# Loading the K cache in runs of 32 KB per partition instead of 16 KB, in a decode kernel that streams its KV cache

## The chip, the cores and the metric

The kernel runs on one core of one Trainium2 chip. The metric is device time in microseconds (us), the median of several executions. Most executions of one kernel agree within 0.3%. Each run is compared with the kernel before as measured beside it, on the same chip.

Engine names: PE is the matrix engine (PEld its weight loads), DVE, ACT and POOL the other compute engines, SP the engine whose queue issues nearly all loads. A core has 16 DMA engines; "DMA" in a profile means these together. L417 is line 417 of the kernel file.

## The reference

One decode step of a transformer block: adaLN modulation, attention of one query row over a cache of 65,536 positions (32 query heads, 4 KV heads, head size 128), output projection, and a GEGLU FFN. Cut to what matters here:

```python
q = (h @ wq)                                  # 1 x 4096: 32 heads of 128
scores = einsum('bhqd,bhkd->bhqk', q, k) * 128 ** -0.5
p = softmax(scores)
o = einsum('bhqk,bhkd->bhqd', p, v)           # k, v: [1, 4, 65536, 128] bf16, each shared by 8 query heads
```

K and V are 67 MB each, the weights another 51 MB. Every byte is read once, so the kernel is a stream of loads with arithmetic beside it. Softmax doesn't care in which order positions are visited, as long as K and V are visited alike.

## The kernel before

Partition p of the SBUF holds 512 consecutive positions of a KV head. The attention has 32 steps. Each takes 64 positions of every partition, which is a run of 64 x 128 x 2 bytes = 16 KB per partition, 2 MB per load. There are ten SBUF buffers of that size ("slots"): K uses 0 to 3, V uses 4 to 7; slots 8 and 9 serve weights only.

```python
SLOT = 8192          # bf16 elements of a partition: 16 KB
NSLOT = 10
SITES = 4            # K buffers, and V buffers
CH = 64              # positions of a partition in a step
...
    for i in range(NC + 2):                                  # NC = 32 steps
        if i < NC:
            j_k[i] = plan_load(kv_src(kh, i), kv_view, i % SITES, kfill[i % SITES])
        if i >= 2:
            j = i - 2
            j_v[j] = plan_load(kv_src(vh, j), kv_view, SITES + j % SITES, vfill[j % SITES])
```

Loads are issued in this planned order and never overtake each other. A load is issued when the work that last used its buffer has ended:

```python
def issue_ready():
    while issued[0] < len(loads):
        j = loads[issued[0]]
        if j.prev is not None:
            if j.prev.freed is None:
                return
            SP.wait(j.prev.freed)
        sp.dma_start(j.view, j.src).then_inc(j.tok[0], 16)
        issued[0] += 1
```

A step i on PE transposes the K of step i (`T`, 4 groups of 16), multiplies the K of step i-1 with the query (`QK`), and multiplies the probabilities of step i-2 with their V (`PV`):

```python
def T(b):
    ...
    if b == 0:
        pwait(kfill[s], i, it)               # this step's K has landed
    ...                                      # 16 transposes into kt_ps (L417)
    if b == NB - 1:
        release(j_k[i], pt[("T", i, b)])     # K buffer free after the last transpose

def PV(q):
    j = i - 2
    ...
    if q == 0:
        pwait(vfill[s], j, it)               # V of step i-2 has landed
    ...                                      # 16 products into b7 (L481)
    if q == NB - 1:
        release(j_v[j], pt[("PV", j)])       # V buffer free

T(0); QK(0); T(1); QK(1); PV(0); T(2); QK(2); QK(3)      # one step (written on
PV(1); T(3); PV(2); MT(); PV(3); MB()                    # separate lines in the kernel)
```

PE runs the steps in a hardware loop of four; every wait shown is on a semaphore that counts up.

## Time and profile before

| what | before |
|---|---|
| time, median | 444.28 us (444.04 to 444.35, 5 runs) |
| span in the profile | 442.7 us |
| bytes read from HBM | 185.60 MB |
| rate from 95 to 340 us | 431 GB/s |
| DMA packets | 15,392 |

The page of the kernel before (slices are 40 equal parts of the span, a digit is the busy share in tenths; then packets, the queue, the chain of waits by engine, and two rows of the issues: loads, KB of each, median us from issue to landing):

```profile
DMA  8999999999999999999999999999999999999994
GB/s 329 429 423 426 434 431 426 429 427 421 432 429 432 426 427 437 432 429 428 434 434 430 429 429 433 431 434 429 429 434 431 432 429 428 423 424 424 427 425 177
DMA packets 15392, 186.08 MB, mean 420 GB/s; under 512 B 1536, under 2 KB 1536, under 8 KB 3840
...
q1 hardware_dynamic: 15328, 185.61, 98.5%
...
DMA 75%; PE 20%; issue 2%; DVE 1%; SPq 1%; ACT 1%
...
slot<-in_A_k_cache_dram SPq DMA_DIRECT2D x32, 2048.0 KB, 29.6
slot<-in_A_v_cache_dram SPq DMA_DIRECT2D x32, 2048.0 KB, 33.2
```

The windows view of the kernel before, for the attention stretch (busy us of each engine, then PE's granted clock, the DMA share and the rate):

```profile
core 0: us, PE busy (x) PEld busy (x) DVE busy (x) ACT busy (x) POOL busy (x), PEclk, DMA share, GB/s
95.00:340.00 245.00, 222.87 (x4900) 218.07 (x4899) 121.02 (x189) 110.11 (x425) 0.00 (x0) 0.79 1.01 431
```

The waits of PE in the kernel before, and the waits of SP's own queue (total us, times, longest):

```profile
PE b L481 <- DMA slot<-in_A_v_cache_dram: 20.9, 15, 2.1
...
PE kt_ps L417 <- DMA slot<-in_A_k_cache_dram: 3.0, 1, 3.0
```

```profile
SPq L212 <- PE kt_ps L417: 250.2, 30, 19.3
SPq L212 <- PE b L481: 45.5, 29, 11.0
```

The reading: the DMA engines are full from the second slice to the last but one. PE is busy in 91% of the attention stretch, which looks close, but it is PE that waits for V. The 250 us that SP waits for transposes look like a bottleneck and are the opposite: SP waits to issue loads *far ahead*. A K load of 2 MB takes 4.9 us at 431 GB/s, yet lands 29.6 us after its issue, because about five older loads are queued in front of it. I call the work that is still queued when a load is issued the **reserve**.

### The profile page before, as it was taken

How to read it: one execution, taken by the hardware profiler on the slowest of the kernel's cores; microseconds unless marked ns; L12 is line 12 of the kernel's file. 1: busy time of each engine (PE TensorE's matmuls, PEld its weight loads, DVE VectorE, ACT ScalarE, POOL GpSimd, SP SyncE). 2: the span in 40 equal slices, each digit the busy share in tenths (PEclk: the TensorE clock that was granted, in tenths of full speed). 3: DMA queues.
4: the chain of work that ended last, by engine and by line, in shares of the span. 5: the costliest groups of instructions: out<-in, count | busy, mean ns of one | idle time of the engine just before them, and what ended most of it. 6: DMA issues, size and time to landing. Idle time of an engine off the chain costs nothing.

```text
span 442.7 us, 16779 instructions
## 1 busy us (share of the span) xinstructions
PE 335.0 (76%) x7849; PEld 325.2 (73%) x7849; DVE 164.8 (37%) x282; ACT 143.1 (32%) x548; POOL 3.8 (1%) x21
## 2 busy tenths in 40 slices
PE   1333468898979899989899988979898974654434
PEld 1333458898979899979799987969898964654434
DVE  1000046544536445544644644554544443210000
ACT  1000013444444333634533453543343562000000
POOL 2000000000000000000000000000000000000000
PEclk9999999867788956967955996895967785555555
DMA  8999999999999999999999999999999999999994
GB/s 329 429 423 426 434 431 426 429 427 421 432 429 432 426 427 437 432 429 428 434 434 430 429 429 433 431 434 429 429 434 431 432 429 428 423 424 424 427 425 177
DMA packets 15392, 186.08 MB, mean 420 GB/s; under 512 B 1536, under 2 KB 1536, under 8 KB 3840
## 3 DMA queue, kind: packets, MB, share of 16 engines
q1 hardware_dynamic: 15328, 185.61, 98.5%
q8 instruction: 25, 0.41, 0.3%
q14 instruction: 7, 0.06, 0.0%
q10 hardware_dynamic: 32, 0.00, 0.0%
HBM read 185.60 MB, written 0.00 MB: 419 GB/s over the span
## 4 chain that ended last, share of the span: by engine, by line
DMA 75%; PE 20%; issue 2%; DVE 1%; SPq 1%; ACT 1%
DMA slot<-in_A_v_cache_dram 55%; PE kt_ps L417 9%; DMA slot<-in_A_wq_dram 8%; DMA slot<-in_B_w_up_dram 6%; DMA slot<-in_B_w_down_dram 6%; PE b L481 5%; PE sc_ps L437 3%; PE kt_ps L316 1%; SPq L212 1%; PE b L461 1%; ACT p_sb L547 1%; PE b L451 1%; DVE kt_sb L612 0%; PE b L621 0%; DVE zs L597 0%
## 5 line engine op out<-in xcount | busy, mean ns | idle before, releaser
L417 PE MATMUL kt_ps<-ident,slot 128*128 128x128 bf16 x2048 | 171.9, 252 | 4.9 <-DMA slot<-in_A_k_cache_dram 3.0
L516 DVE COPY kt_sb<-kt_ps 128x2048 bf16<-128x2048 bf16 x96 | 117.5, 1225 | 100.0 <-PE kt_ps L417 99.7
L417 PEld LDWEIGHTS kt_ps<-ident,slot 128*128 128x128 bf16 x2048 | 148.6, 114 | 6.6 <-issue 4.2
L516 ACT ACTIVATE kt_sb<-kt_ps 128x2048 bf16<-128x2048 bf16 x32 | 60.1, 1878 | 217.7 <-PE kt_ps L417 217.7
L481 PE MATMUL b<-p_sb,slot 128*128 128x8 bf16 x2048 | 71.0, 167 | 29.5 <-DMA slot<-in_A_v_cache_dram 20.9
L481 PEld LDWEIGHTS b<-p_sb,slot 128*128 128x128 bf16 x2048 | 65.1, 100 | 32.2 <-DMA slot<-in_A_v_cache_dram 22.2
L547 ACT ACTIVATE p_sb<-sc_ps,mneg 128x64 bf16<-128x64 f32 x256 | 83.6, 560 | 5.7 <-DVE mneg L542 5.7
L547 ACT ACTIVATION_READ_ACCUMULATOR p_sb<-sc_ps,mneg 128x1 f32 x256 | 77.2, 364 | 0.0
L437 PE MATMUL sc_ps<-q_buf,kt_sb 128*128 128x8 bf16 x2048 | 67.4, 167 | 0.1
L437 PEld LDWEIGHTS sc_ps<-q_buf,kt_sb 128*128 128x128 bf16 x2048 | 65.1, 100 | 0.2 <-issue 0.2
L316 PE MATMUL kt_ps<-h_col,slot 128*128 128x1 bf16 x448 | 16.2, 172 | 16.9 <-DMA slot<-in_B_w_up_dram 9.1
L316 PEld LDWEIGHTS kt_ps<-h_col,slot 128*128 128x128 bf16 x448 | 15.6, 118 | 17.6 <-DMA slot<-in_B_w_up_dram 9.4
L316 PE MATMUL sc_ps<-s_col,slot 128*128 128x1 bf16 x384 | 11.5, 165 | 15.8 <-DMA slot<-in_w_mod_dram 15.8
L535 DVE TENSOR_REDUCE m_col<-sc_ps 128x8 f32<-128x512 f32 x32 | 21.8, 681 | 4.4 <-PE sc_ps L437 4.4
L316 PEld LDWEIGHTS sc_ps<-s_col,slot 128*128 128x128 bf16 x384 | 11.0, 105 | 16.4 <-DMA slot<-in_w_mod_dram 16.4
L540 DVE TENSOR_REDUCE mg<-b 8x1 f32<-8x128 f32 x32 | 8.9, 279 | 34.4 <-PE b L451 34.4
L316 PE MATMUL sc_ps<-h_col,slot 128*128 128x1 bf16 x256 | 7.4, 165 | 12.6 <-DMA slot<-in_A_wq_dram 12.6
L316 PEld LDWEIGHTS sc_ps<-h_col,slot 128*128 128x128 bf16 x256 | 7.1, 104 | 12.9 <-DMA slot<-in_A_wq_dram 9.3
L461 PE MATMUL b<-negi,mg 8*128 8x8 f32 x64 | 15.0, 304 | 0.4 <-DVE mg L540 0.4
L461 PEld LDWEIGHTS b<-negi,mg 8*128 8x128 f32 x64 | 12.0, 233 | 2.6 <-DVE mg L540 0.6
L316 PE MATMUL kt_ps<-u_col,slot 128*128 128x1 bf16 x224 | 6.6, 165 | 9.6 <-DMA slot<-in_B_w_down_dram 9.6
L316 PEld LDWEIGHTS kt_ps<-u_col,slot 128*128 128x128 bf16 x224 | 6.3, 104 | 9.9 <-DMA slot<-in_B_w_down_dram 6.8
(74 smaller groups left out, 63.2 us busy)
## 6 DMA issues: line engine op xcount, KB each, us to landing
slot<-in_A_k_cache_dram SPq DMA_DIRECT2D x32, 2048.0 KB, 29.6
slot<-in_A_v_cache_dram SPq DMA_DIRECT2D x32, 2048.0 KB, 33.2
slot<-in_w_mod_dram SPq DMA_DIRECT2D x8, 1536.0 KB, 19.0
slot<-in_A_wq_dram SPq DMA_DIRECT2D x4, 2048.0 KB, 37.0
slot<-in_A_wo_dram SPq DMA_DIRECT2D x4, 2048.0 KB, 34.7
slot<-in_B_w_gate_dram SPq DMA_DIRECT2D x4, 1792.0 KB, 39.4
slot<-in_B_w_up_dram SPq DMA_DIRECT2D x4, 1792.0 KB, 29.0
slot<-in_B_w_down_dram SPq DMA_DIRECT2D x3, 2048.0 KB, 30.4
```

What stands on the lines that cost most here:

```text
L212: sp.dma_start(j.view, j.src).then_inc(j.tok[0], 16)
L316: ins = pe.matmul(bank[:, j:j + 1], w, rhs[:, k0 + kk:k0 + kk + 1], start=first, stop=True, skip_group_check=True,)
L417: ins = pe.transpose(kt_ps[:, half * 2048 + t * P:half * 2048 + (t + 1) * P], j_k[i].view[:, b * TB + t, :], ident[:, :],)
L437: ins = pe.matmul(sc_ps[:, base + n * REP:base + (n + 1) * REP], kt_sb[:, j % 2, n, :], q_buf[:, j % SITES, :], start=True, stop=True,)
L451: ins = pe.transpose(b6[0:REP, 32:32 + P], m_col[:, j % 2, :], identf[:, :]) if emit else None
L461: ins = pe.matmul(b6[:, 256:256 + REP], mg8[:, j % 2:j % 2 + 1].to_broadcast([REP, P]), negi[:, :], start=True, stop=True,)
L481: ins = pe.matmul(b7[:, s * REP:(s + 1) * REP], j_v[j].view[:, n, :], p_sb[:, s, n, :], start=(n == 0), stop=(n == CH - 1),)
L516: ev[i % SITES][b].done(act.activation(dst, src, ACT.Copy) if E_ is AC else dve.tensor_copy(dst, src))
L535: m1[s].done(dve.tensor_reduce(m_col[:, j % 2, :].unsqueeze(2), scv, AX.X, ALU.max))
L540: m2[s].done(dve.tensor_reduce(mg8[:, j % 2:j % 2 + 1], b6[0:REP, 32:32 + P], AX.X, ALU.max))
L547: ins = act.activation(p_sb[:, s, :, h], scv[:, h, :], ACT.Exp, bias=mneg[:, j, h:h + 1], scale=scale, accum_out=z_all[:, j, h:h + 1],)
```

## The change

The intent is fewer, longer runs: each K load now fetches two steps' worth, 32 KB per partition, 4 MB, into two adjoining slots. K then has two such buffers instead of four single ones. V stays at 16 KB and four buffers. The diff, cut to its core:

```diff
+KU = 2
-    slots = [nc.alloc_sbuf_tensor(f"slot{i}", [P, SLOT], dt.bfloat16) for i in range(NSLOT)]
+    slot_all = nc.alloc_sbuf_tensor("slots", [P, NSLOT * SLOT], dt.bfloat16)
+    slots = [slot_all[:, i * SLOT:(i + 1) * SLOT] for i in range(NSLOT)]
...
-    kfill = [Site(nc, f"kfill{i}", 16) for i in range(SITES)]
+    kfill = [Site(nc, f"kfill{i}", 16) for i in range(SITES // KU)]
...          (plan_load takes nslot, and waits for the last users of all its slots)
-            if i < NC:
-                j_k[i] = plan_load(kv_src(kh, i), kv_view, i % SITES, kfill[i % SITES])
+            if i < NC and i % KU == 0:
+                j_k[i] = plan_load(kv_src(kh, i, KU), flat(KU * CH, DH), i % SITES, kfill[i % SITES // KU], KU)
...
-                if b == 0:
-                    pwait(kfill[s], i, it)
+                if b == 0 and i % KU == 0:
+                    pwait(kfill[s // KU], i, it)
...
-                            j_k[i].view[:, b * TB + t, :],
+                            j_k[i - i % KU].view[:, i % KU * CH + b * TB + t, :],
...
-                if b == NB - 1:
-                    release(j_k[i], pt[("T", i, b)])
+                if b == NB - 1 and i % KU == KU - 1:
+                    release(j_k[i - i % KU], pt[("T", i, b)])
```

No instruction of a compute engine is added, removed or moved. What changes is the length of a run and the moment at which a K buffer comes free: after the second step of a pair.

More of the change, by code (lines that the diff above doesn't have):

```diff
@@ L184, in bass_adaLN_cond__gqa_block_cached__geglu_ffn__decode_kernel, with plan_load @@
     loads = []
-    def plan_load(src, view_fn, slot, site=None):
+    def plan_load(src, view_fn, slot, site=None, nslot=1):
         if site is not None:
@@ L193, in plan_load @@
             tok = (fill[slot], 16 * nfill[slot])
-        job = Job(view_fn(slots[slot]), tok, slot)
+        job = Job(view_fn(slot_all[:, slot * SLOT:(slot + nslot) * SLOT]), tok, slot)
         job.src = src
         job.freed = None
-        job.prev = last_job[slot]
-        last_job[slot] = job
+        job.prev = []
+        for t in range(slot, slot + nslot):
+            if last_job[t] is not None and last_job[t] not in job.prev:
+                job.prev.append(last_job[t])
+            last_job[t] = job
         loads.append(job)
@@ L207, in issue_ready @@
             j = loads[issued[0]]
-            if j.prev is not None:
-                if j.prev.freed is None:
-                    return
-                SP.wait(j.prev.freed)
+            if any(q.freed is None for q in j.prev):
+                return
+            SP.wait(*(q.freed for q in j.prev))
             sp.dma_start(j.view, j.src).then_inc(j.tok[0], 16)
@@ L236, in emit_all, with kv_src @@
         vh = [A_v_cache[0, g].rearrange("(p n) d -> p n d", p=P) for g in range(Hkv)]
-        def kv_src(h, i):
+        def kv_src(h, i, n=1):
             g, cc = divmod(i, NCH)
-            return h[g][:, cc * CH:(cc + 1) * CH, :]
-        kv_view = flat(CH, DH)
+            return h[g][:, cc * CH:(cc + n) * CH, :]
         head = [8, 9, 0, 1, 2, 4, 3, 5, 6, 7, 8, 9]
@@ L248, in emit_all @@
         for i in range(NC + 2):
-            if i < NC:
-                j_k[i] = plan_load(kv_src(kh, i), kv_view, i % SITES, kfill[i % SITES])
+            if i < NC and i % KU == 0:
+                j_k[i] = plan_load(kv_src(kh, i, KU), flat(KU * CH, DH), i % SITES, kfill[i % SITES // KU], KU)
             if i >= 2:
                 j = i - 2
-                j_v[j] = plan_load(kv_src(vh, j), kv_view, SITES + j % SITES, vfill[j % SITES])
+                j_v[j] = plan_load(kv_src(vh, j), flat(CH, DH), SITES + j % SITES, vfill[j % SITES])
         tail = iter([8, 9, 0, 1, 2, 4, 3, 5, 6, 7, 8, 9] + [0, 1, 2, 4, 3, 5, 6, 7])
```

## The prediction

> **What bounds the kernel now.** The DMA engines. The slices show them 90% or more busy in 38 of 40, and the windows give 431 GB/s from 95 to 340 us (attention). 185.6 MB at that rate take 431 of the 442.7 us. PE is busy in 91% of that stretch (222.9 of 245 us, mean granted clock 0.79): near, but not the limit. The waits show PE held by V landings 15 times (20.9 us); the queue's own waits show SP waiting 250 us for transposes to free K buffers, which is slack: a K load takes 29.6 us from issue to landing, though 2 MB take 4.9 us at 431 GB/s, so five earlier loads are queued ahead of it. By the issue times, a step's last transpose ends 4 to 7 us after its V landed, with 29 us of loads behind that V: the queue keeps at least 22 us of work.
>
> **What the change does.** K packets grow from 16 to 32 KB: 2048 for 4096, 16 loads fewer. The trace's packet records give the median time of a packet: 159 ns for 4 KB, 272 for 7 KB, 309 for 8 KB, 460 for 12 KB, 611 for 16 KB: a line of 8.3 ns plus 0.0368 ns a byte. A 32 KB packet should take 1214 ns (estimate); the gain is 2048 x 8.3 ns over 16 engines, 1.06 us, and sixteen 9 ns semaphore packets on each engine, 0.14 us: together 1.2 us, 0.27%, all on the critical path, because the queue is full. The Trainium skill, "DMA: Bandwidth & Descriptors", section "Where 436 GB/s comes from", puts the ceiling at 435 GB/s. The trace agrees: the slope is 435 GB/s, and at 16 KB only 1.4% is overhead; doubling it has little left to win.
>
> **What it costs.** K buffers come free in pairs, after the second step's last transpose. Only one K pair and two V loads (19.5 us) are then behind the V just landed, and the transposes end about 7 us (full clock) to 11 us (half clock) after it. The reserve falls from 22 to 8 to 12 us: still no idle DMA. The first transpose waits for the first pair, 4.9 us later (63.6 instead of 58.8 us); the next pair is then issued at about 75 us, and what is queued lasts to about 82 us, the thinnest place. PE's work is unchanged, and so is the DMA-bound end.
>
> **Predicted time:** 443.1 us, range 442.0 to 445.0; faster by over 2% 0.01, within 2% 0.97, slower by over 2% 0.02.
>
> **What would show each step right.** Packets fall from 15392 to about 13088; those of 32 KB take about 1214 ns. The rate from 95 to 340 us rises by 1 to 2 GB/s. DMA stays at 9 in the slices, also at 70 to 90 us. A K load lands about 21 us after issue, for twice the bytes. PE's waits for K landings rise from one (3.0 us) to about one per pair, without moving the end. The chain of waits stays about 75% DMA.
>
> **What would make it wrong.** PE's clock at half for many steps in a row: such a step is about 10.9 us (chain: 1.73 us for 16 transposes, 0.41 to 0.43 for 16 others) against 9.75 us of DMA, so three or more slow pairs would use up the reserve and the DMA would idle. A hole at the start. Or 32 KB runs cut into 16 KB packets: no change.

## The result, and the profile after

The changed kernel took 443.42 us (443.29 to 443.68, 5 runs) against 444.28 us. The ratio is 0.9983, with a 95% interval of 0.9971 to 0.9995. A ratio here is the mean time of one kernel's fast runs over the mean of the other's in the same rounds, so not quite the ratio of the medians quoted. Executions over 1.5% slower than the fastest of the same kernel are left out of the means. In means the gain is 0.76 us, in medians 0.86 us. All outputs are right.

The page of the changed kernel, the same lines:

```profile
DMA  8999999999999999999999999999999999999994
GB/s 330 425 426 426 449 429 418 444 412 436 427 423 444 418 445 416 442 433 424 438 426 447 421 438 425 433 442 421 437 423 445 426 429 429 422 424 425 424 425 182
DMA packets 13088, 186.08 MB, mean 421 GB/s; under 512 B 1280, under 2 KB 1280, under 8 KB 3584
...
q1 hardware_dynamic: 13024, 185.60, 98.4%
...
DMA 53%; PE 40%; issue 3%; ACT 2%; DVE 1%; SPq 1%
...
slots<-in_A_k_cache_dram SPq DMA_DIRECT2D x16, 4096.0 KB, 19.4
slots<-in_A_v_cache_dram SPq DMA_DIRECT2D x32, 2048.0 KB, 26.7
```

The windows view of the changed kernel, same stretch:

```profile
95.00:340.00 245.00, 222.64 (x4962) 217.71 (x4959) 123.28 (x192) 114.05 (x442) 0.00 (x0) 0.81 1.01 432
```

The waits of PE in the changed kernel, and of SP's queue:

```profile
PE kt_ps L419 <- DMA slots<-in_A_k_cache_dram: 15.9, 6, 7.9
...
PE b L483 <- DMA slots<-in_A_v_cache_dram: 9.6, 11, 1.3
```

```profile
SPq L216 <- PE kt_ps L419: 289.0, 15, 37.6
```

The median time of one packet by its size, from the packet records of the two traces:

```
bytes    before: count, median ns    after: count, median ns
 4,096       256, 159                    256, 159
 7,168      2048, 272                   2048, 272
 8,192      1806, 309                   1805, 309
12,288      1024, 460                   1024, 460
16,384      8729, 611                   4633, 611
32,768         0                        2048, 1213
```

What to see: a 32 KB run is one packet, not two of 16 KB. The number of packets is exactly the one predicted. The DMA is as full as before: counting the packet records that are open (begun and not ended) at each moment, there are never fewer than 16 from 40 to 370 us, in either kernel. (The records don't name their engine, so an idle one could hide only while another has two open.) The rate in the attention stretch rises from 431 to 432 GB/s. K loads land sooner after their issue (19.4 us, for twice the bytes): the queue in front of them is shorter. And the chain of waits now goes through PE for 40% of the span instead of 20%, although PE bounds nothing. That number is a trap, taken up below.

The thinnest place, by the prediction, was the start: the first transpose must wait for a whole pair. The timeline of PE in the kernel before, then in the changed kernel (start, length, ..., idle time just before), and SP's next K issue in the changed one:

```profile
58.78 4.25 PE L417 MATMUL kt_ps<-ident,slot 128*128 128x128 bf16 x48 [3.04 <-DMA slot<-in_A_k_cache_dram]
```

```profile
63.64 4.61 PE L419 MATMUL kt_ps<-ident,slots 128*128 128x128 bf16 x48 [7.86 <-DMA slots<-in_A_k_cache_dram]
```

```profile
75.65 0.33 SPq L216 DMA_DIRECT2D slots<-in_A_k_cache_dram  x1
```

PE starts 4.9 us later, and the third K load is issued at 75.65 us, while by the prediction's estimate what was queued lasts to about 82 us. No slice there falls below 9, and with never fewer than 16 packets open there is no hole.

So the direction, the place and the absence of a cost came out as predicted. What is left open is the size. The summed packet times fell by 1.23 us over 16 engines (437.96 to 436.73 us), as predicted; the time fell by only 0.6 to 0.9 us. Was a part of the gain given back somewhere, or was it never there?

### The profile page after: what moved, and what is told of

It is laid out like the page before. It is cut to its first block, busy times and chain, and to the rows that moved or that the text cites. A ratio compares the mean times of both kernels' runs of the same rounds, so it can differ in the third digit from the quotient of the medians.

```text
span 441.8 us, 16747 instructions
## 1 busy us (share of the span) xinstructions
PE 333.3 (75%) x7849; PEld 323.6 (73%) x7849; DVE 164.9 (37%) x282; ACT 142.9 (32%) x548; POOL 3.7 (1%) x21
## 2 busy tenths in 40 slices
DMA packets 13088, 186.08 MB, mean 421 GB/s; under 512 B 1280, under 2 KB 1280, under 8 KB 3584
## 4 chain that ended last, share of the span: by engine, by line
DMA 53%; PE 40%; issue 3%; ACT 2%; DVE 1%; SPq 1%
DMA slots<-in_A_v_cache_dram 27%; PE kt_ps L419 22%; DMA slots<-in_A_k_cache_dram 9%; PE b L483 8%; PE sc_ps L439 7%; DMA slots<-in_B_w_up_dram 6%; DMA slots<-in_B_w_down_dram 6%; DMA slots<-in_w_mod_dram 5%; PE b L463 2%; ACT p_sb L549 1%; SPq L216 1%; ACT kt_sb L518 1%; PE b L453 1%; PE kt_ps L318 0%; DVE kt_sb L518 0%
## 5 line engine op out<-in xcount | busy, mean ns | idle before, releaser
L419 PE MATMUL kt_ps<-ident,slots 128*128 128x128 bf16 x2048 | 171.4, 251 | 18.7 <-DMA slots<-in_A_k_cache_dram 15.9
L419 PEld LDWEIGHTS kt_ps<-ident,slots 128*128 128x128 bf16 x2048 | 147.8, 114 | 20.5 <-issue 10.2
L483 PE MATMUL b<-p_sb,slots 128*128 128x8 bf16 x2048 | 70.4, 167 | 22.2 <-DMA slots<-in_A_v_cache_dram 9.6
L483 PEld LDWEIGHTS b<-p_sb,slots 128*128 128x128 bf16 x2048 | 64.7, 99 | 24.8 <-issue 13.5
L318 PE MATMUL kt_ps<-h_col,slots 128*128 128x1 bf16 x448 | 16.0, 172 | 10.0 <-DMA slots<-in_B_w_up_dram 7.0
L318 PE MATMUL sc_ps<-s_col,slots 128*128 128x1 bf16 x384 | 11.5, 165 | 15.8 <-DMA slots<-in_w_mod_dram 15.8
L318 PEld LDWEIGHTS kt_ps<-h_col,slots 128*128 128x128 bf16 x448 | 15.5, 118 | 10.5 <-DMA slots<-in_B_w_up_dram 7.4
L318 PEld LDWEIGHTS sc_ps<-s_col,slots 128*128 128x128 bf16 x384 | 11.1, 105 | 16.4 <-DMA slots<-in_w_mod_dram 16.4
L318 PE MATMUL sc_ps<-h_col,slots 128*128 128x1 bf16 x256 | 7.4, 165 | 12.6 <-DMA slots<-in_A_wq_dram 12.6
L318 PEld LDWEIGHTS sc_ps<-h_col,slots 128*128 128x128 bf16 x256 | 7.1, 104 | 12.9 <-DMA slots<-in_A_wq_dram 9.3
## 6 DMA issues: line engine op xcount, KB each, us to landing
slots<-in_A_k_cache_dram SPq DMA_DIRECT2D x16, 4096.0 KB, 19.4
```

Of the source, the lines that this page charges most:

```text
L318: ins = pe.matmul(bank[:, j:j + 1], w, rhs[:, k0 + kk:k0 + kk + 1], start=first, stop=True, skip_group_check=True,)
L419: ins = pe.transpose(kt_ps[:, half * 2048 + t * P:half * 2048 + (t + 1) * P], j_k[i - i % KU].view[:, i % KU * CH + b * TB + t, :], ident[ ...
L483: ins = pe.matmul(b7[:, s * REP:(s + 1) * REP], j_v[j].view[:, n, :], p_sb[:, s, n, :], start=(n == 0), stop=(n == CH - 1),)
```

## The experiments

Two questions. First: what does a packet really cost, and is it the packets at all? *Packet theory*: the time follows the number of packets. Rivals: it follows the number of loads (sixteen fewer); or the paired buffers cost something that the longer packets pay for; or 0.2% is noise. Second: how much reserve does the kernel need? *Reserve theory*: pairing is free only as long as the queue doesn't run dry.

### The changed kernel again

No edit; in a later job, on the same chip as K in pairs of 16 KB, the runs of 8 KB and V in 32 KB as well.

> The changed kernel again, on the chip of the two runs after it. Packet theory (the time follows the summed packet times, about 8.3 ns per packet over 16 engines, and the queue never runs dry): 1.2 us under before, so about 443.1 us. Rival (noise, or luck with PE's clock): anything within 0.3 us of before as often as not.

Measured: 443.61 us (443.50 to 443.81, 5 runs) against 444.18 us (443.98 to 444.43, 11 runs): 0.57 us less. No run of the changed kernel is as slow as the fastest run of the one before, so this isn't noise, although the interval of this job's ratio, 0.9974 to 1.0000, only just ends at "no change". It is half of the 1.2 us expected.

### K in the same pairs, but two runs of 16 KB

```diff
         def kv_src(h, i, n=1):
             g, cc = divmod(i, NCH)
-            return h[g][:, cc * CH:(cc + n) * CH, :]
+            m, r = divmod(cc, KU)
+            w = CH * DH
+            src = h[g].rearrange("p (r x) -> p r x", r=KU)
+            if n == KU:
+                return src[:, :, m * w:(m + 1) * w]      # two runs of 16 KB, 64 KB apart
+            return src[:, r, m * w:(m + 1) * w]          # V of a step: the same positions
```

> K in the same 16 loads of 4 MB with the same paired buffers, but each partition's 32 KB in two separate runs of 16 KB (another split of the sequence over the steps; V follows it, the result stays right). Packet theory: packets back to about 15,136 (before's 15,392 less 256 semaphore packets), only the sixteen semaphore packets are saved, 0.14 us: about 444.1 us. Rival (the gain comes from fewer loads, not from longer packets): the time stays at that of the changed kernel, about 443.4. Second rival (paired buffers cost time that the longer packets pay for): above 444.5.

Measured: 444.21 us (443.96 to 444.25, 5 runs; before beside it 444.18), ratio 0.9999 with an interval of 0.9986 to 1.0012. The packets, from its page:

```profile
DMA packets 15136, 186.08 MB, mean 421 GB/s; under 512 B 1280, under 2 KB 1280, under 8 KB 3584
...
slots<-in_A_k_cache_dram SPq DMA_DIRECT2D x16, 4096.0 KB, 19.4
```

The loads, buffers and landing times are those of the changed kernel (19.4 us), and the gain is gone with the long packets. So it was the packets, not the number of loads; and the pairing costs nothing that this interval could show, because it stands alone in this run and leaves the time where it was. Compared with the changed kernel on the same chip, 2048 packets more cost 444.21 - 443.61 = 0.60 us, or 0.60 x 16 / 2048 = 4.7 ns per packet. That is a rough figure: from the means it is 4.1, and the spread of the runs, 0.3 us, is worth 2.3 ns. The sixteen loads saved, with their 256 semaphore packets, show no gain of their own (444.21 against 444.18 us).

### Shorter runs: 8 KB and 4 KB for K and V

In the kernel before, with NR = 2 or 4:

```diff
+NR = 2
...
         def kv_src(h, i):
             g, cc = divmod(i, NCH)
-            return h[g][:, cc * CH:(cc + 1) * CH, :]
+            w = CH * DH // NR
+            return h[g].rearrange("p (r x) -> p r x", r=NR)[:, :, cc * w:(cc + 1) * w]
```

> The kernel before, with each 2 MB load of K and V in two runs of 8 KB a partition instead of one of 16 KB; same loads, same buffers. Packet theory: 8192 packets more, 8192 x 8.3 ns / 16 = 4.25 us: 448.5 us, packets of 309 ns. Rival (the length of a packet does not matter at these sizes): 444.3.

> As the last, in four runs of 4 KB a partition. Packet theory: 24,576 packets more than before, 12.75 us: 457.0 us, packets of 159 ns. Rival (length does not matter): 444.3. If HBM reads of short runs cost more than the packet line says: above 458.

Measured: 446.64 us with 8 KB (4 runs; before beside it 444.18), 2.46 us more; 451.49 us with 4 KB (4 runs; before beside it 444.08), 7.41 us more. Windows of the 8 KB run, then of the 4 KB run:

```profile
95.00:340.00 245.00, 224.65 (x4856) 220.00 (x4854) 120.26 (x187) 109.95 (x425) 0.00 (x0) 0.77 1.01 427
```

```profile
95.00:340.00 245.00, 224.60 (x4841) 220.01 (x4839) 119.35 (x186) 107.03 (x409) 0.00 (x0) 0.76 1.02 421
```

The page of the 4 KB run:

```profile
DMA packets 39968, 186.08 MB, mean 414 GB/s; under 512 B 1536, under 2 KB 1536, under 8 KB 36608
...
q1 hardware_dynamic: 39904, 185.61, 99.8%
```

This settles the size. 2.46 us x 16 / 8192 packets is 4.8 ns; 7.41 x 16 / 24,576 is 4.8 ns (5.0 and 4.8 from the means). The time grows in proportion to the packets, by 4.8 ns each, not by the 8.3 ns read from the packet records. (Shorter runs also lie elsewhere in memory. That wasn't tested by itself, but above, runs of 16 KB read two at a time, 64 KB apart, took as long as single ones.) The records double-count: the share of the DMA queue is 98.5% of 442.7 us in the kernel before (436.1 us) and 99.8% of 449.8 us with 4 KB (448.9 us), a growth of 12.8 us, while the time grew by 7.4 us. The trace shows why. Sixteen engines can't be more than fully busy, yet the records that are open at one moment number 17 or more in 10% of the attention stretch in the kernel before, and in 33% with 4 KB (and never fewer than 16). So the records of neighbouring packets overlap. Added up over the whole span, what lies above 16 is 3.5 us before and 9.1 us with 4 KB. This growth of 5.6 us, plus the 7.1 us by which the span grew, makes up the 12.8 us to within 0.1 us.

It also answers the question left open. From the kernel before to the changed one, the records fell by 1.23 us; 0.60 us of that is overlap (3.52 less 2.92 us), and the other 0.63 us is what the engines were really spared. The missing half was never there, and nothing was given back. With 4.8 ns, the change should gain 2048 x 4.8 / 16 = 0.61 us; with 0.14 us for the sixteen semaphore packets it would be 0.76 us. The two measurements are 0.57 and 0.86 us, which can't tell these apart, so the 0.14 us is not shown.

The Trainium skill, "DMA: Bandwidth & Descriptors", section "Why small descriptors are slow (HBM only)", names two costs: about 3 cycles per packet inside the DMA engine, and 32 bytes of descriptor data per operation. If the cycles are those of the 850 MHz that its section "Where 436 GB/s comes from" gives for the fabric, and a run is one packet and one operation in that page's sense, an estimate from these two sections is 3.5 ns plus 32 bytes at 27.2 bytes a ns, 1.2 ns: together 4.7 ns. The runs agree with the sum (4.8 ns with 8 and 4 KB); none of them separates the two parts.

### Giving K back one step later: the changed kernel, and the one before

```diff
 (changed kernel)
-                if b == NB - 1 and i % KU == KU - 1:
+                if b == NB - 1 and i % KU == 0 and i > 0:
+                    release(j_k[i - KU], pt[("T", i, b)])
+                if b == NB - 1 and i == NC - 1:
                     release(j_k[i - i % KU], pt[("T", i, b)])

 (kernel before)
-                if b == NB - 1:
+                if b == NB - 1 and i > 0:
+                    release(j_k[i - 1], pt[("T", i, b)])
+                if b == NB - 1 and i == NC - 1:
                     release(j_k[i], pt[("T", i, b)])
```

> The changed kernel with each K pair given back one step later (after the last transpose of the next step). Reserve theory (8 to 12 us of queued loads left in the changed kernel): one step is more than that, so the DMA runs dry once per pair; [...]10 to 34 us more, about 460 us, DMA share below 1.00 in the windows. Rival (the paired buffers have far more reserve than that, or none is needed): 443.4.

> The same delay of one step in the kernel before, buffer by buffer. Reserve theory: 22 us of reserve less 9.8 leaves 12: no change, 444.3 us, K loads landing about 20 us after issue instead of 29.6. Rival (any delay of the K loads costs time): above 446.

Measured: the changed kernel with the late release took 480.48 us (478.01 to 482.64, 3 fast runs; a fourth, 485.81, counts as slow and is left out; before beside it 444.08), ratio 1.0815. The kernel before with the same delay took 444.28 us (444.22 to 444.51), ratio 1.0005. The page of the former and its window from 95 to 340 us, then the K issues of the latter:

```profile
DMA  8999997888888999799989999899989999999996
...
slots<-in_A_k_cache_dram SPq DMA_DIRECT2D x16, 4096.0 KB, 12.1
```

```profile
95.00:340.00 245.00, 213.82 (x4326) 209.23 (x4322) 106.72 (x168) 99.86 (x382) 0.00 (x0) 0.70 0.91 380
```

```profile
slot<-in_A_k_cache_dram SPq DMA_DIRECT2D x32, 2048.0 KB, 19.8
```

The kernel before hardly notices a step's delay (9.8 us): its K loads land 19.8 us after issue instead of 29.6, and the queue is still full. The changed kernel doesn't have that much to give. Its DMA falls to 7 and 8 tenths and to 380 GB/s in the attention stretch, and in 4.8% of that stretch no packet is open at all; 4 MB then land 12.1 us after issue, which is little more than the 9.7 us that they take at 431 GB/s. The size was more than expected (36.4 us against 10 to 34): a pair took 22.0 us on average (K issues at 84.95 and 371.22 us, thirteen pairs apart), against the 19.5 us that its loads take at 431 GB/s, and PE's mean clock in the stretch was 0.70 where it had been 0.81.

The dry queue gives a yardstick, which is an estimate. If about 12.1 us is what 4 MB need without a queue, and about 12.1 - 4.9 = 7.2 us what 2 MB need, then the reserve of any run is its landing time less that: 22.4 us before, 7.3 us in the changed kernel.

### V in runs of 32 KB as well

```diff
-            if i >= 2:
+            if i >= 2 and i % KU == 0:
                 j = i - 2
-                j_v[j] = plan_load(kv_src(vh, j), flat(CH, DH), SITES + j % SITES, vfill[j % SITES])
+                j_v[j] = plan_load(kv_src(vh, j, KU), flat(KU * CH, DH), SITES + j % SITES, vfill[j % SITES // KU], KU)
...      (V waited for in the first step of a pair, given back after the second)
```

> V too in runs of 32 KB, two buffers of a pair each. Packet theory: another 2048 packets and 16 loads fewer than in the changed kernel, another 1.2 us: about 442.2 us, 10,784 packets. But the reserve of the queue falls by up to 4.9 us more (the first step of a pair must wait for both V), to about 3 us. Reserve theory: if that is too little, the DMA share falls below 1.00 in some windows and the time is 443 to 447.

Measured: 446.08 us, and scattered: 443.53 to 449.03 in six runs (before beside it 444.18), ratio 1.005 with an interval of 1.0015 to 1.0085. The K and V issues of its page, then two of its windows:

```profile
slots<-in_A_k_cache_dram SPq DMA_DIRECT2D x16, 4096.0 KB, 16.3
slots<-in_A_v_cache_dram SPq DMA_DIRECT2D x16, 4096.0 KB, 23.8
```

```profile
160.00:180.00 20.00, 17.09 (x445) 16.57 (x442) 12.09 (x17) 11.30 (x51) 0.00 (x0) 1.00 0.98 419
340.00:360.00 20.00, 20.00 (x360) 19.73 (x358) 8.71 (x14) 8.85 (x34) 0.00 (x0) 0.52 0.98 410
```

With half the packets of K and V gone, this kernel should be the fastest so far; it is slower than the kernel before. Its reserve is 16.3 - 12.1 = 4.2 us, and the DMA runs dry in places. The share of 0.98 alone wouldn't show it, because a packet counts in the window where it starts: the changed kernel, which has no hole, also has 0.98 from 60 to 80 us. The count of open packets does: it falls under 16 at about 100, 120, 159, 199, 238 and 355 us, for 0.7 to 4.0 us each. It never falls under 10 in these holes: some engines are out of work while the others still have some. Two causes are possible: too little reserve, or 32 KB packets of V that are slow in themselves. Two runs tell them apart. The first keeps the pairs of both and splits each into two runs of 16 KB, as for K above; the second has V in 32 KB runs and K single, with the order K, K, V pair:

```diff
 (pairs of K and of V in two runs of 16 KB each: the edit of the second experiment, and)
+            if i >= 2 and i % KU == 0:
+                j = i - 2
+                j_v[j] = plan_load(kv_src(vh, j, KU), flat(KU, CH * DH), SITES + j % SITES, vfill[j % SITES // KU], KU)

 (V in runs of 32 KB, K in runs of 16 KB)
+            if i < NC:
+                j_k[i] = plan_load(kv_src(kh, i), flat(CH, DH), i % SITES, kfill[i % SITES])
+            if i >= 3 and i % KU == 1:
+                j = i - 3
+                j_v[j] = plan_load(kv_src(vh, j, KU), flat(KU * CH, DH), SITES + j % SITES, vfill[j % SITES // KU], KU)
```

> The buffers and loads of the run with V in 32 KB runs too (pairs of K and of V, 16 loads each of 4 MB), but each partition's 32 KB in two runs of 16 KB. Reserve theory (that run was slow because pairs of both leave the queue too little work): just as slow and as scattered, 445 to 450 us, DMA share below 1.00 in some windows. Rival (V packets of 32 KB are themselves slow): about 444.0.

> V in runs of 32 KB (pairs), K in runs of 16 KB buffer by buffer. Packets as in the changed kernel (13,088). Packet theory with the cost per packet that the runs with 8 and 4 KB showed (4.8 ns, not 8.3): 2048 x 4.8 / 16 + 0.14 = 0.76 us under before, 443.4 us. Reserve theory: K loads are issued step by step, so the reserve is 12 us or more, no idle DMA, runs within 0.3 us of each other. Rival (V in 32 KB is slow): 445 or more.

Measured: the pairs of both in 16 KB runs took 446.92 us (444.92 to 448.14, 6 runs; before beside it 444.23), ratio 1.006: as slow and about as scattered, with packets of 16 KB, and with the same kind of holes (at about 100, 159, 238, 278 and 338 us). V alone in 32 KB runs took 443.66 us (443.21 to 443.74, 5 runs) against 444.23 us (11 runs), ratio 0.9983, the same gain as K's. So 32 KB packets of V are not slow; pairs of both are. The K issues of the first, then of the second:

```profile
slots<-in_A_k_cache_dram SPq DMA_DIRECT2D x16, 4096.0 KB, 16.8
```

```profile
slots<-in_A_k_cache_dram SPq DMA_DIRECT2D x32, 2048.0 KB, 19.0
```

### Both in 32 KB runs, with the transposes first

If reserve is what's missing, it can be won back without touching the loads. A K buffer waits for its last transpose, and that stood behind the step's first product with V, so behind a V landing. This edit lets all four transpose groups go first. The same edit in the kernel before is the control.

```diff
             QK(1)
-            PV(0)
             T(2)
             QK(2)
             QK(3)
-            PV(1)
             T(3)
+            PV(0)
+            PV(1)
             PV(2)
```

> K and V in runs of 32 KB, with the four transpose groups of a step ahead of its first product with V, so that K buffers come free without waiting for V. Reserve theory: the last transpose of a pair ends about 4 us earlier after the landing of V, the reserve grows from 4 to about 8 us, and the DMA stays busy: two times 0.76 us under before, 442.7 us, runs close together. Rival (the loss is not a matter of reserve): still 444 to 449.

> The same order of groups in the kernel before, as a control. Its queue already has 22 us of reserve: no change, 444.2 us. Rival (the order itself makes PE faster and that pays): below 443.5.

Measured: both in 32 KB runs with transposes first took 442.81 us (442.56 to 442.93, 5 runs) against 444.23 us (11 runs), ratio 0.9969 with an interval of 0.9956 to 0.9982. The control took 444.22 us (443.89 to 444.38), ratio 1.0000. The K issues on the page of the first, its windows, and PE's clock in tenths on the page of both in 32 KB without and with the new order:

```profile
slots<-in_A_k_cache_dram SPq DMA_DIRECT2D x16, 4096.0 KB, 19.2
```

```profile
95.00:340.00 245.00, 226.77 (x4896) 221.69 (x4897) 120.59 (x187) 112.88 (x432) 0.00 (x0) 0.79 1.00 432
```

```profile
PEclk9999999769896599669959778995997588555555
```

```profile
PEclk9999999886788966689868879668788677555555
```

The reserve went from 4.2 to 7.1 us, the scatter and the holes vanished (never fewer than 16 packets open from 40 to 370 us), and the gain is 1.42 us where twice 0.76 was expected. The order by itself gains nothing (the control). This is the fastest version, 0.3% under the kernel before.

One rival needs a word, because the order changed a second thing: PE's clock. The clock records of both in 32 KB show, from 80 to 365 us, 10 stretches at half clock with a median length of 13.7 us; with transposes first there are 24, with a median of 3.4 us. Shorter slow stretches could also spare the queue. But the reserve grew at equal clock: where the mean clock of the 20 us before a K issue was 0.66, the load landed after 13.8 to 15.2 us (three loads) with the old order and after 18.6 and 18.7 us with the new one. So the order did win reserve; whether the shorter stretches helped too is not separated.

The runs by reserve (landing time of a K load less 12.1 us for a load of 4 MB or 7.2 us for one of 2 MB; without the repeat, the shorter runs and the control of the order). "Expected" is the time before, less 4.8 ns per packet over 16 engines and 9 ns per load saved (the last term, at most 0.29 us, is the one that is not shown):

| run | reserve, us | expected | measured | range of the runs |
|---|---|---|---|---|
| before (first job) | 22.4 | 444.28 | 444.28 | 0.31 |
| before, K given back late | 12.6 | 444.08 | 444.28 | 0.29 |
| V in 32 KB | 11.8 | 443.47 | 443.66 | 0.53 |
| the change (K in 32 KB, first job) | 7.3 | 443.52 | 443.42 | 0.39 |
| K in pairs of 16 KB | 7.3 | 444.04 | 444.21 | 0.29 |
| both in 32 KB, transposes first | 7.1 | 442.71 | 442.81 | 0.37 |
| both in pairs of 16 KB | 4.7 | 443.94 | 446.92 | 3.22 |
| both in 32 KB | 4.2 | 442.66 | 446.08 | 5.50 |
| the change, K given back late | 0 by definition | 443.32 | 480.48 | 4.63 |

Down to a median reserve of about 7 us nothing is lost; at 4 to 5 us three are. Why the limit isn't at zero: the reserve varies from step to step, and the engines don't run dry together. A step's PE time varies with PE's clock (16 transposes took 0.91 us at full clock and 1.73 us at half in the chain of the kernel before). With both in 32 KB, the K loads after the first two landed after 13.8 to 18.0 us, so the poorest pair had 1.7 us of reserve where the median is 4.2; in the changed kernel the poorest had 5.1. Five of the six holes came during a half-clock stretch of 10 us or more, or within 6 us after it; of seven such stretches two left no hole to speak of. So the slow stretches are where the queue runs short, but the exact course of each hole is not settled, nor is why some runs of one kernel are hit more than others (their mean clocks, 0.775 to 0.799, don't order them).

## Why the prediction was right or wrong

The prediction was 443.1 us, the result 443.42 us, inside the range; the class "within 2%" was right. That alone proves little: the range, 442.0 to 445.0, also holds the time of the kernel before. The steps say more. Point by point:

- **The DMA bounds the kernel, and the gain lies on the critical path: right.** With the queue full, the time moved with the number of packets (runs of 4, 8, 16 and 32 KB), 4.8 ns per packet with 8 and 4 KB, and 4.1 to 4.7 between K in runs of 16 and 32 KB, where the runs' spread is half of the difference. The rate from 95 to 340 us rose by 1 GB/s, as predicted.
- **Packets fall to 13,088, and a 32 KB run is one packet of about 1214 ns: right** (13,088, and 1213 ns).
- **"the gain is 2048 x 8.3 ns over 16 engines, 1.06 us": the term that was mis-sized.** It measured 2048 x 4.8 / 16 = 0.61 us. The step that failed is taking "a line of 8.3 ns plus 0.0368 ns a byte" from packet records as if they stood end to end. They overlap: records summed grew by 12.8 us in the 4 KB run, the time by 7.4; of the 1.23 us by which they fell in the change, 0.60 was overlap. The 0.14 us for semaphore packets is not shown either way. The time fell inside the range all the same, because the range is wider than the whole gain. A check was at hand before: the windows view gave a DMA share of 1.01, and 16,384 bytes at 431 GB/s over 16 engines are 608 ns from packet to packet, 3 ns less than the record's 611.
- **The pairing costs nothing: right**, shown by the pairs of 16 KB (ratio 0.9999). The reserve fell from 22 to 7.3 us, a little under the 8 to 12 predicted; a K load lands after 19.4 us instead of about 21.
- **The start: right.** First transpose at 63.64 us (63.6), next pair issued at 75.65 us (about 75), no hole.
- **"PE's waits for K landings rise ... to about one per pair": half right.** The total rose to 15.9 us but in six waits, not sixteen, one of them the 7.9 us at the start; the waits for V fell from 20.9 to 9.6 us.
- **"The chain of waits stays about 75% DMA": wrong**, 53% now and PE 40%. PE bounds neither kernel, as the queue never runs out of work. A likely reading is that the chain goes back from a load to the PE work that let it be issued, so that with a shorter queue more of each round trip is spent in PE. But it is not settled: K in pairs of 16 KB has the same landing time (19.4 us) and a chain of 63% DMA and 31% PE. A share of that chain is no measure of what limits.
- **What could have made it wrong**: the queue running dry was the right danger. It didn't occur in the change, but it did one step further (both in 32 KB), at a median of 4 us of reserve.

## What to carry to other kernels

When the DMA is full and runs are already 16 KB, doubling them is worth about 5 ns per packet saved over 16 engines, here 0.13 to 0.19%, and the same bytes in coarser buffers cost reserve: watch the time from issue to landing, less the time that a load takes on an idle queue, and keep a median of some 7 us of it in a kernel whose PE step times vary like this one's. If coarser buffers use it up, look for what a buffer's release stands behind; moving the transposes ahead of the products with V gave back 3 us of reserve and turned a loss into the best version. And don't add up packet durations from a trace: count how many are open at once, or change the number of packets and divide.

## What the Trainium skill lacked or had wrong

- "DMA: Bandwidth & Descriptors", section "Why small descriptors are slow (HBM only)": it gives the per-packet cost in cycles, and the page has no measured time of a packet's overhead in a full queue. Here it is 4.8 ns per packet and engine from 4 to 16 KB, and 4.1 to 4.7 ns between 16 and 32 KB. For loads issued from SP the page has a single rate, for rows of 4 KB, and no series by run length; here the attention stretch ran at 421, 427 and 431 GB/s with runs of 4, 8 and 16 KB, and 432 GB/s with both in 32 KB.
- "HBM Reference", section "Specifications (TRN2)": it gives about 425 GB/s for a core that streams alone. This kernel held 431 GB/s over 245 us, so for runs of 16 KB the figure is 1.4% low.
- No page says that packet records of a trace overlap, so that their sum exceeds the time: here a DMA share of 1.01 to 1.02, 17 or more records open at once on 16 engines in 10 to 33% of the attention stretch, and an apparent cost of 8.3 ns per packet where 4.8 ns is the real one.
- No page gives the reserve a load queue needs. "DMA: Bandwidth & Descriptors", section "Rules for kernel authors", asks for at least 1 MiB per DMA for the best bandwidth; going from loads of 2 MB to 4 MB with the same runs gained nothing (444.21 against 444.18 us), and with pairs of both K and V it cost 2.7 us, at 4.7 us of reserve.
